# A diffusion transformer block on one core: one load for batch 1's x, one multiply moved up on VectorE, one K step split around a scale group

## The chip, the cores and the metric

The kernel runs on one core of a Trainium2 chip. Its metric is the device time of one execution in microseconds. Before the change, eight runs gave a median of 244.0 us (243.49 to 245.54).

## The reference, cut to what matters

```python
mod = (_silu(c) @ w_mod).reshape(B, 6, 1, D)
shift_a, scale_a, gate_a, shift_m, scale_m, gate_m = [mod[:, i] for i in range(6)]
h = _layernorm(x) * (1 + scale_a) + shift_a
qkv = (h @ wqkv).reshape(B, N, 3, H, Dh)
...
attn = _softmax(jnp.einsum('bqhd,bkhd->bhqk', q, k) * Dh ** (-0.5))
a = jnp.einsum('bhqk,bkhd->bqhd', attn, v).reshape(B, N, D) @ wo
x = x + gate_a * a
h2 = _layernorm(x) * (1 + scale_m) + shift_m
m = _gelu(h2 @ w_fc1) @ w_fc2
return x + gate_m * m
```

Here B is 2, N is 256, D is 1152, H is 2 and the hidden width F is 4608. Everything is bfloat16. All weights together are 50 MB, and each is read once.

## The kernel before, in words

The 512 tokens are four tiles of 128 rows: tiles 0 and 1 are batch 0, tiles 2 and 3 are batch 1. Row p of a partition holds tokens 2p and 2p+1 of a batch, so the two tiles of one batch are the two halves of 4608 contiguous bytes per partition in HBM. D is nine chunks of 128 columns.

All x and weight loads are issued from SyncE's queue (SP), in program order, and start with x in the order tile 0, 1, 3, 2 (L85 and L86), then alternate between column groups of the scale weights `w_scale_a` (L107) and rows of the key weights `w_k` (L104). Transfers take turns on eight completion semaphores, so each one waits for the transfer eight places before it.

The change lies in the first stage, up to about 24 us, which computes the K projection while its inputs still arrive:

- **Warming up.** TensorE runs float32 matmuls on zeros (`warm`, L173).
- **Layer-norm statistics.** Tiles 0 and 2 are done on ScalarE (`act_stats`, L204: two passes with an accumulator); tiles 1 and 3 on VectorE (`stats_piece`, L193: three pieces, then an aggregate, L195). VectorE runs strictly in the order written: tile 1's pieces, the squared mean of tile 0 (L211), tile 3's first piece, tile 0's variance (`act_var`, L222), tile 3's other pieces and aggregate, and then the normalisation `norm1` (L231) of tiles 1, 0 and 3. GpSimd makes the reciprocal square roots of tiles 0, 1 and 3 (`pool_rsqrt`, L327); ScalarE that of tile 2 by logarithm and exponential (`ln_exp_rsqrt`, L227 and L228).
- **Scale.** `scale_group` (L245) multiplies one or more column chunks of `w_scale_a` by silu(c): nine tiny matmuls per chunk. Chunks 0 and 1 are called `pm0` and `pm1`. `scale_add` adds one (L253 on ScalarE, L255 on VectorE).
- **Transposing and modulating.** `transpose_x` (L262) turns normalised chunks with TensorE into PSUM. `modulate` multiplies by the scale on the way to `hT0` (on VectorE L268, or for chunk 0 of batch 0 at L356; on ScalarE L270). For chunks 4 and up, both batches are one PSUM tile; VectorE does batch 0, and ScalarE then does batch 1.
- **K steps.** `k_step(k, c0, c1, m0, m1)` (L278) adds chunk k's contribution to six PSUM accumulators m = 0 to 5, for token columns c0 to c1. For k from 3 on (L387 to L393) the loop does, at k = 3, 5 and 7, the scale group of the next chunks, then the transposes of chunk k+1, then the K step with 512 columns.

After the K steps come panels 6 to 8 of K (L307), the shift (L405), Q (L510), attention, V (L588), the output projection (L679) and the two MLP matmuls (L732 and L788). Every engine's instructions keep the order of the program text, because the kernel ties each to the one before it.

Of the kernel before, what the change touches and what calls it, by code (L numbers as in the profile page):

```python
# [19 lines left out]
def kernel(  # L20
# [11 lines left out]
    nc = tc.nc  # L32
    B, N, D = x.shape
# [4 lines left out]
    T = B * N  # L38
    NT = T // P
    TPB = N // P  # L40
# [19 lines left out]
    def acc_tile(shape, name, dt=FP32):  # L60
        return psum.tile(shape, dt, name=name, tag="acc", bufs=6)
# [5 lines left out]
    x_v = x.rearrange("b (p l) d -> p b l d", l=TPB)  # L67
# [14 lines left out]
    x_sb = act.tile([P, NT, D], BF16, name="x_sb", tag="x_sb")  # L82
    c_sb = act.tile([B * KD, P], BF16, name="c_sb")
    nc.scalar.dma_start(c_sb[:], c_v)
    for t in (0, 1, 3, 2):  # L85
        nc.sync.dma_start(x_sb[:, t, :], x_v[:, t // TPB, t % TPB, :])  # L86

    zeros = const.tile([P, T], BF16, name="zeros")
    nc.vector.memset(zeros[:], 0.0)
# [55 lines left out]
    hT0 = aT  # L145
# [74 lines left out]
    def act_var(t):  # L220
        one = slice(t, t + 1)
        nc.vector.scalar_tensor_tensor(  # L222
            mv1[:, t, 1:2], dsq[:, one], 1.0 / D, dm2[:, one], op0=ALU.mult, op1=ALU.add
        )
# [5 lines left out]
    def norm1(t, c0, c1):  # L230
        nc.vector.tensor_scalar(  # L231
            xns[t][:, c0:c1], x_sb[:, t, c0:c1], mv1[:, t, 0:1], rstd1[:, t:t + 1],
            op0=ALU.subtract, op1=ALU.mult,
        )
# [4 lines left out]
    def scale_group(k0, k1, tile_of=aux_tile):  # L239
        pm = tile_of([P, k1 - k0, B], "pm")  # L240
        for j in range(k0, k1):
            if j == 0:
                nc.tensor.matmul(pm[:, 0, :], ones_row[:], ones_row[:, 0:B], start=True, stop=False)
            for k in range(KD):
                nc.tensor.matmul(  # L245
                    pm[:, j - k0, :], w_scale_a[:, k, j * P:(j + 1) * P], sT[:, k, 0:B],
                    start=(k == 0 and j > 0), stop=(k == KD - 1),
                )
        return pm

    def scale_add(pm, k0, k1, eng="d"):
        if eng == "a":
            nc.scalar.activation(scale_a[:, k0:k1, :], pm[:], ACT.Identity, bias=ones[:])  # L253
        else:
            nc.vector.tensor_scalar_add(scale_a[:, k0:k1, :], pm[:], 1.0)  # L255

    def transpose_x(ks, ts, pt=None, j0=0):
        if pt is None:
            pt = aux_tile([P, len(ks), len(ts) * P], "pt", BF16)
        for j, t in enumerate(ts, j0):  # L260
            for i, k in enumerate(ks):
                nc.tensor.transpose(pt[:, i, j * P:(j + 1) * P], xns[t][:, k * P:(k + 1) * P], ident[:])  # L262
        return pt
# [10 lines left out]
    def k_step(k, c0=0, c1=T, m0=0, m1=KM1):  # L274
        for m in range(m0, m1):
            if k == 0 and c0 == 0:
                pk[m] = acc_tile([P, T], "pk")
            nc.tensor.matmul(  # L278
                pk[m][:, c0:c1], w_k[:, k, m * P:(m + 1) * P], hT0[:, k, c0:c1],
                start=(k == 0 and c0 == 0), stop=(k == KD - 1), skip_group_check=True,  # L280
            )
# [33 lines left out]
    def both(pt, k):  # L315
        for b, e in enumerate("da"):
            modulate(pt, 0, k, b, b * N, e)
# [32 lines left out]
    pt_a = transpose_x([0, 1], BT[0])  # L350
    act_sq_mean(2)
    act_mean(2)
    norm1(3, 0, CUT)
    pm0, pm1 = [scale_group(k, k + 1, acc_tile) for k in range(2)]
    act_var(2)
    nc.vector.tensor_scalar_mul(hT0[:, 0, 0:N], pt_a[:, 0, :], pm0[:, 0, 0:1])  # L356
    scale_add(pm1, 1, 2, "a")
    modulate(pt_a, 1, 1, 0, 0, "d")
    ln_exp_rsqrt(rstd1[:, 2:3], mv1[:, 2, 1:2])
# [25 lines left out]
    k_step(2, 0, N)  # L385
    k_step(2, N, T)
    for k in range(3, KD):  # L387
        if k in (3, 5, 7):
            k1 = min(k + 3, KD)
            scale_add(scale_group(k + 1, k1), k + 1, k1)  # L390
        if k < KD - 1:
            both(transpose_x([k + 1], range(NT)), k + 1)
        k_step(k)  # L393
    for m in range(KM1):
        k_evac(m)

# [446 lines left out]
```

## Time and profile before

| What | Value |
|---|---|
| median of eight runs | 244.0 us (243.49 to 245.54) |
| profiled execution, its own time | 244.49 us |
| its span, first to last instruction | 242.7 us |
| TensorE busy | 237.6 us (98%) |
| VectorE, ScalarE, GpSimd busy | 91.4, 59.7, 29.0 us |
| bytes read from HBM | 50.14 MB |
| mean granted TensorE clock | 1.000 |

Times inside an execution are microseconds from the start of the span. In the timeline, each row is a run of equal instructions on one engine: start, length, engine, source line, operation, output<-inputs, shapes, count, and in brackets the idle time before the first of them with what ended it. In the chain of waits, each row is start, length and what held the end of the program at that time, followed back from the last instruction. "PEld" is TensorE's weight load, "SPq" the issue of a transfer on SyncE's queue.

### The profile page before, as it was taken

The page shows a single profiled execution, that of the slowest core. Times are in us where ns is not written, and L with a number is a line of the kernel's source. Part 1 is how long each engine was busy: PE and PEld are TensorE (multiplying, and loading weights), DVE is VectorE, ACT ScalarE, POOL GpSimd, SP SyncE. Part 2 cuts the span into 40 slices and gives each one's busy share as a digit, 9 for nine tenths or more (in the row PEclk, how much of TensorE's full clock was granted, in tenths as well). Part 3 has the DMA queues.
Part 4 walks back from the last instruction along what each step waited for, and adds up shares of the span by engine and source line. Part 5 has one row for each costly group of instructions (what it writes and reads, how often), then busy time and mean ns, then how long its engine had stood idle before and what let it go on. Part 6 is the DMA issues. An engine that isn't in the chain of part 4 may idle for free.

```text
span 242.7 us, 3999 instructions
## 1 busy us (share of the span) xinstructions
PE 237.6 (98%) x1701; PEld 145.4 (60%) x1701; DVE 91.4 (38%) x193; ACT 59.7 (25%) x120; POOL 29.0 (12%) x48
## 2 busy tenths in 40 slices
PE   8999999999999999999999999999999999999994
PEld 5685444466567665888854444444665665665674
DVE  4652442318416578831001999960010000000001
ACT  6632332307214032672422223332000000000000
POOL 2400000001400333200000000001121121111111
PEclk9999999999999999999999999999999999999999
DMA  6999999998599999239999999999200000000000
GB/s 189 321 318 277 365 367 391 390 393 280 96 320 397 389 375 143 39 66 329 389 392 392 346 326 304 258 326 302 93 20 16 20 16 16 20 16 16 29 23 16
DMA packets 48781, 53.29 MB, mean 220 GB/s; under 512 B 9587, under 2 KB 36475, under 8 KB 48763
## 3 DMA queue, kind: packets, MB, share of 16 engines
q1 hardware_dynamic: 41312, 50.14, 62.3%
q10 hardware_dynamic: 6939, 1.71, 4.9%
q0 software_dynamic: 512, 1.19, 1.7%
q8 instruction: 13, 0.21, 0.4%
q14 instruction: 5, 0.04, 0.1%
HBM read 50.14 MB, written 1.19 MB: 212 GB/s over the span
## 4 chain that ended last, share of the span: by engine, by line
PE 90%; SPq 4%; DMA 3%; issue 0%; DVE 0%; DVEq 0%
PE pacc L732 29%; PE pacc L788 29%; PE pacc L679 7%; PE pacc L588 7%; PE pq L510 7%; DMA w_scale_a<-in_w_mod_dram 3%; SPq L104 3%; PE pk L307 2%; PE pk L278 2%; PE pa L628 2%; PE ps_s L545 2%; PE pn L405 2%; SPq L107 1%; SPq L86 1%; PE pg L487 0%; PE pm L245 0%
## 5 line engine op out<-in xcount | busy, mean ns | idle before, releaser
L732 PE MATMUL pacc<-hT,w_f 128*128 128x256 bf16 (+1 forms) x432 | 70.5, 326 | 0.0
L788 PE MATMUL pacc<-w_f,gT 128*128 128x384 bf16 (+2 forms) x468 | 70.5, 314 | 0.0
L788 PEld LDWEIGHTS <-gT 128*128 128x128 bf16 x468 | 44.4, 98 | 26.2
L732 PEld LDWEIGHTS <-w_f 128*128 128x128 bf16 x432 | 42.2, 98 | 27.6
L794 DVE TENSOR_TENSOR tmp<-pacc,gate 128x384 f32<-128x384 f32 (+2 forms) x13 | 6.9, 527 | 65.6 <-PE pacc L788 57.0
L764 ACT ACTIVATE gT<-pacc 128x512 bf16<-128x512 f32 x24 | 14.4, 598 | 32.6 <-PE pacc L732 32.6
L458 DVE SCALAR_TENSOR_TENSOR part<-w_gate_m,s,part 128x1152 f32<-128x1152 bf16 x16 | 21.3, 1410 | 0.0
L796 POOL TENSOR_TENSOR o_sb<-tmp,x 128x384 bf16<-128x384 f32 (+1 forms) x12 | 11.7, 974 | 53.8 <-DVE tmp L794 53.8
L679 PE MATMUL pacc<-w_o,big 128*128 128x384 bf16 x108 | 17.9, 326 | 0.0
L510 PE MATMUL pq<-hT,w_q 128*128 128x512 bf16 x81 | 17.8, 379 | 0.0
L588 PE MATMUL pacc<-w_v,hT 128*128 128x384 bf16 x108 | 17.7, 326 | 0.0
L588 PEld LDWEIGHTS <-hT 128*128 128x128 bf16 x108 | 10.5, 98 | 7.1 <-issue 0.3
L679 PEld LDWEIGHTS <-big 128*128 128x128 bf16 x108 | 10.4, 98 | 7.2 <-issue 0.4
L510 PEld LDWEIGHTS <-w_q 128*128 128x128 bf16 x81 | 7.8, 97 | 9.5
L278 PE MATMUL pk<-big,w_k 128*128 128x256 bf16 (+1 forms) x72 | 13.2, 326 | 0.1
L685 POOL TENSOR_TENSOR x<-tmp,x_sb 128x384 f32<-128x384 f32 x8 | 7.3, 915 | 27.1 <-DMA w_scale_m<-in_w_mod_dram 15.2
L456 DVE TENSOR_SCALAR part<-w_gate_m,s 128x1152 f32<-128x1152 bf16 x2 | 1.5, 816 | 22.4 <-DMA w_gate_m<-in_w_mod_dram 22.4
L480 POOL DMA_DIRECT2D gates_dram<-nat_v x2 | 1.1, 536 | 67.6 <-DVE nat_v L478 67.6
L278 PEld LDWEIGHTS <-w_k 128*128 128x128 bf16 x72 | 6.7, 98 | 3.8 <-issue 0.4
L173 PE MATMUL pwarm<-zeros 128*128 128x256 f32 x20 | 7.7, 556 | 1.2 <-DVE eps_t L93 1.2
L753 ACT ACTIVATE gT<-pacc 128x512 bf16<-128x512 f32 x12 | 6.5, 599 | 9.1 <-PE pacc L732 9.1
L501 POOL DMA_DIRECT2D gates_dram<-nat x4 | 2.3, 587 | 50.6 <-DVE nat L498 49.9
(101 smaller groups left out, 166.4 us busy)
## 6 DMA issues: line engine op xcount, KB each, us to landing
w_f<-in_w_fc_dram SPq DMA_DIRECT2D x12, 864.0 KB, 14.9
w_f<-in_w_fc_dram SPq DMA_DIRECT2D x3, 1728.0 KB, 8.0
w_f<-in_w_fc_dram SPq DMA_DIRECT2D x2, 2592.0 KB, 17.2
w_gate_a<-in_w_mod_dram SPq DMA_DIRECT2D x3, 864.0 KB, 11.8
w_v<-in_wqkv_dram SPq DMA_DIRECT2D x3, 864.0 KB, 13.9
w_o<-in_wo_dram SPq DMA_DIRECT2D x3, 864.0 KB, 14.1
w_shift_m<-in_w_mod_dram SPq DMA_DIRECT2D x3, 864.0 KB, 8.2
w_scale_m<-in_w_mod_dram SPq DMA_DIRECT2D x3, 864.0 KB, 13.7
```

The costliest lines, as they stand in the source:

```text
L104: nc.sync.dma_start(w_k[:, k0:k1, c0:c1], wqkv_v[:, k0:k1, D + c0:D + c1])
L173: nc.tensor.matmul(dst[:, 0:T // 2], zeros32[:, 0:P], zeros32, start=True, stop=True)
L278: nc.tensor.matmul(pk[m][:, c0:c1], w_k[:, k, m * P:(m + 1) * P], hT0[:, k, c0:c1], start=(k == 0 and c0 == 0), stop=(k == KD - 1), skip_g ...
L458: nc.vector.scalar_tensor_tensor(part[:, b, :], wg[:, k, :], s32[:, k, b:b + 1], part[:, b, :], op0=ALU.mult, op1=ALU.add,)
L510: nc.tensor.matmul(pq[m][:], w_q[:, k, m * P:(m + 1) * P], hT[:, k, :], start=(k == 0), stop=(k == KD - 1), skip_group_check=True,)
L588: nc.tensor.matmul(pacc[:], hT[:, k, t * P:(t + 1) * P], w_v[:, k, pnl * PW:(pnl + 1) * PW], start=(k == 0), stop=(k == KD - 1),)
L679: nc.tensor.matmul(pacc[:], aT[:, k, t * P:(t + 1) * P], w_o[:, k, c0:c1], start=(k == 0), stop=(k == KD - 1),)
L685: (nc.gpsimd if pool_add else nc.vector).tensor_tensor(x1[:, t, c0:c1], tmp[:], x_sb[:, t, c0:c1], op=ALU.add)
L732: nc.tensor.matmul(dst, w_f1[m // KD][:, k, ml * P:(ml + 1) * P], hT[:, k, c0:c1], start=start, stop=(k == KD - 1), **kw,)
L764: nc.scalar.activation(gT[:, m, :], pacc[:], ACT.Gelu_apprx_tanh)
L788: nc.tensor.matmul(pacc[:], gT[:, kk, t * P:(t + 1) * P], w_f2[j][:, r, c0 - n * PW:c0 - n * PW + cw], start=(kk == 0), stop=(kk == KF - 1),)
L796: (nc.vector if last else nc.gpsimd).tensor_tensor(o_sb[:], tmp[:], x1[:, t, c0:c0 + cw], op=ALU.add)
```

## The change

Three edits in the first stage:

1. Tiles 2 and 3 of x, which were two loads of 288 KB (tile 3 first), become one load of 576 KB with 4608 contiguous bytes per partition. Tiles 0 and 1 keep their loads and their place.
2. On VectorE the multiply of chunk 0 of batch 0 (L356) is put before tile 2's variance (L222) instead of after it.
3. In the K loop, the matmuls of K step 5 for accumulators 0 and 1 are put before the scale group of chunks 6 and 7; those for accumulators 2 to 5 stay where they were.

```diff
-    for t in (0, 1, 3, 2):
-        nc.sync.dma_start(x_sb[:, t, :], x_v[:, t // TPB, t % TPB, :])
+    for t in range(TPB):
+        nc.sync.dma_start(x_sb[:, t, :], x_v[:, 0, t, :])
+    nc.sync.dma_start(x_sb[:, TPB:2 * TPB, :], x_v[:, 1, :, :])
...
     pm0, pm1 = [scale_group(k, k + 1, acc_tile) for k in range(2)]
+    nc.vector.tensor_scalar_mul(hT0[:, 0, 0:N], pt_a[:, 0, :], pm0[:, 0, 0:1])
     act_var(2)
-    nc.vector.tensor_scalar_mul(hT0[:, 0, 0:N], pt_a[:, 0, :], pm0[:, 0, 0:1])
     scale_add(pm1, 1, 2, "a")
...
     for k in range(3, KD):
+        split = 2 if k == 5 else 0
+        k_step(k, 0, T, 0, split)
         if k in (3, 5, 7):
             k1 = min(k + 3, KD)
             scale_add(scale_group(k + 1, k1), k + 1, k1)
         if k < KD - 1:
             both(transpose_x([k + 1], range(NT)), k + 1)
-        k_step(k)
+        k_step(k, 0, T, split)
```

## The prediction

> **What bounds the kernel now.** I read the page's chain of waits first, then that chain in order of time, then TensorE's waits, then the timeline of the first 23 us, because all three edits lie there.
>
> ```profile
> PE 90%; SPq 4%; DMA 3%; issue 0%; DVE 0%; DVEq 0%
> ```
>
> TensorE bounds nine tenths of the span; transfers bound only the start. In order of time, the last stretch that is not TensorE is this:
>
> ```profile
> 11.62 8.41 DMA w_scale_a<-in_w_mod_dram
> 20.03 0.05 issue
> 20.08 0.60 PE pm L245 x18
> ...
> 20.93 1.30 PE pk L278 x6
> ```
>
> The scale weights of chunks 6 and 7 land at 20.03, and TensorE waits for them. After that TensorE waits for no transfer: its list of waits from 24 us on is empty. Any shift of TensorE at 22 us therefore reaches the end undiminished. The waits of its first 40 us:
>
> ```profile
> PE pwarm L173 <- DVE eps_t L93: 1.2, 1, 1.2
> PE pm L245 <- DMA w_scale_a<-in_w_mod_dram: 0.7, 2, 0.3
> ```
>
> Two waits for scale weights, one at 9.67 and one at 20.08. The timeline shows what stands behind each:
>
> ```profile
> 6.30 0.56 DVE L193 BATCH_NORM_STATS2 stats<-x_sb 128x6 f32<-128x384 bf16 x1 [0.17 <-DMA x_sb<-in_x_dram]
> ...
> 6.78 0.14 DVE L222 SCALAR_TENSOR_TENSOR mv<-dsq,dm 128x1 f32<-128x1 f32 x1
> ...
> 7.07 0.73 POOL L327 TENSOR_TENSOR rstd<-mv,neg_half 128x2 f32<-128x2 f32 x1 [0.42 <-DVE mv L222]
> 7.71 1.26 ACT L204 ACTIVATE xn<-x_sb 128x1152 bf16<-128x1152 bf16 x1 [1.31 <-DMA x_sb<-in_x_dram]
> ...
> 8.04 0.67 DVE L231 TENSOR_SCALAR xn<-x_sb,mv,rstd 128x512 bf16<-128x512 bf16 x2
> ...
> 8.85 0.38 PE L262 MATMUL pt<-ident,xn 128*128 128x128 bf16 x4
> ...
> 9.67 0.60 PE L245 MATMUL pm<-sT,w_scale_a 128*128 128x2 bf16 x18 [0.33 <-DMA w_scale_a<-in_w_mod_dram]
> ...
> 10.38 0.26 ACT L253 ACTIVATE scale_a<-pm,ones 128x2 f32<-128x2 f32 x1
> ...
> 10.67 0.30 ACT L227 ACTIVATE rstd<-mv,eps_t 128x1 f32<-128x1 f32 x1
> ...
> 11.30 0.41 DVE L231 TENSOR_SCALAR xn<-x_sb,mv,rstd 128x512 bf16<-128x512 bf16 x1
> ...
> 11.77 0.28 PE L262 MATMUL pt<-ident,xn 128*128 128x128 bf16 x2
> ```
>
> Tile 3 lands at 6.28, tile 2 only at 7.69. VectorE starts tile 3's statistics the moment that tile is there, and everything that batch 0 needs (tile 0's variance, its root on GpSimd, the normalisation of tiles 1 and 0) is queued behind them. `pm0` at 9.67 waits for its weights with the transposes done at about 9.2: that path has some 0.45 us to spare.
>
> **Edit 1, one load for tiles 2 and 3.** It removes one issue (0.43 us, with 0.04 between issues) from SP, so every later issue can come 0.47 earlier. I take that as worth nothing: the issue of `w_k` at 5.42 already lasts 2.89 us, the queue pushing back. What it could give is bounded by 0.47 and, since the engines' share was 0.75 and 0.69 between 5 and 6 us, more nearly by 0.3. The eight-semaphore rotation moves up by one place; the transfers now waited for (c, tiles 0 and 1, then the pair) have landed before their waiters are issued. No wait on SP appears.
>
> It adds a wait: tile 3's statistics now wait for tile 2's bytes too. Call the landing of the pair t. Behind it on VectorE, with the rows' own distances from tile 3's 6.28: tile 0's variance at t+0.50, GpSimd's root at t+0.79 to t+1.52, tile 3's remaining statistics until t+1.76, the normalisation of tiles 1 and 0 until t+2.43, the four transposes from t+2.57, then `pm0` at t+2.95. ScalarE's two passes over tile 2 end at t+2.76, as 10.45 follows 7.69 now, before they are needed. So `pm0` moves from 9.67 to t+2.95: a delay d = t - 6.72. From `pm0` on, the distances stay: the weights of chunk 0 and 1 land 1.93 us after x (9.62 after 7.69), well before t+2.95.
>
> What is t? The same bytes, at the same place of the queue, are all there at 7.69 now. Lower end: the slowest part of tile 1 lands at 4.35 by the trace's semaphore records; 589,824 bytes at the page's best 393 GB/s are 1.50 us, so 5.85. Upper end: tile 3's part on the slowest engine took 1.93 us (4.35 to 6.28); two such are 8.21. The gap between 5.85 and 7.69 is slow packets: single ones of 2304 bytes took 0.4 to 1.2 us between 3.7 and 5.5 us, against some 0.1 us else. Half as many packets may meet fewer. The nearest row is 7.69; I take 7.5, so d = +0.78 (ends -0.87 and +1.49).
>
> The Trainium skill, "DMA: Bandwidth & Descriptors", section "Rules for kernel authors", advises to coalesce small transfers into a large one, and its fit for one transfer (2.0 us + bytes/436e3, an estimate here) would land the pair at about 5.0, issued at 1.63, which would be a gain. The trace disagrees in advance: the four x loads already overlap, landing 0.71, 1.93 and 1.41 us apart. The same page, on why a DMA increments its semaphore by 16, says that only the full count means that all data has landed; that is the rule against this edit.
>
> **Edit 2, the multiply before tile 2's variance.** Its input `pm0` is ready at about 10.15, yet it starts at 10.55, behind the variance that waits until 10.48. Moved up, the first K step could start 0.28 earlier (10.68, when TensorE is free, instead of 10.96). But TensorE then stands at tile 2's transposes, 11.77, which hang on ScalarE: its scale add at 10.38 waits for `pm1`, the logarithm at 10.67 follows it. The variance, now behind the multiply's 0.27 us of occupation, is ready for 10.67 still. Worth 0.00; ends: a gain of 0.16 (what TensorE loses before 11.77, 0.27 between starts instead of 0.11) and a loss of 0.35, the multiply's length, if the logarithm had to wait for all of it.
>
> **Edit 3, two matmuls of K step 5 first.** In these rows TensorE finishes K step 4 and waits:
>
> ```profile
> 18.27 1.46 PE L278 MATMUL pk<-big,w_k 128*128 128x512 bf16 x6
> 20.08 0.60 PE L245 MATMUL pm<-sT,w_scale_a 128*128 128x2 bf16 x18 [0.35 <-DMA w_scale_a<-in_w_mod_dram]
> ...
> 22.28 1.46 PE L278 MATMUL pk<-big,w_k 128*128 128x512 bf16 x6
> ```
>
> Six 512-column matmuls take 1.30 from start to start, so the group could have begun at 19.57: 0.51 lost. Two matmuls of 0.216 fill 0.43 of it; their data (chunk 5, ScalarE done at 19.34) is there. A new wait eats some: chunk 6 is transposed by 20.71 (the last start) and modulated by VectorE, then ScalarE, until 21.86. Between those transposes and K step 6 there were 1.57 us of TensorE work; now 1.14, against 1.21 needed. So edit 3 gains 0.43 - 0.07 = 0.36 where the stall is whole, and costs 0.07 where there is none.
>
> **The sum.** TensorE reaches the group at 19.57 + 0.43 + d. With d = 0.78 that is 20.78, later than the weights' 20.03, so no stall is left. K step 6 starts at 20.78 + 1.84 = 22.62 against 22.28: +0.34. On the profiled execution's own 244.49 this is 244.83.
>
> That execution is 0.49 above the median. Its stall explains such a difference: 15 of the 16 parts of that load had landed by 18.86, and one came 1.17 later, on an engine that read 16 KB of instructions from 17.74 for 1.2 us. A run without that collision has no 0.51 to give back; there the change costs 0.78 + 0.07, and 244.0 becomes 244.85. Both give 244.8.
>
> **The rivals.**
>
> Fewer slow packets: t near 6.9, d = +0.18. Then 244.49 + 0.18 - 0.36 or 244.0 + 0.25: about 244.3, no measurable change. For it: half the packets, and 12 of the 16 parts of tile 2 had landed by 7.05. Against it: the slowest engine decides, and it lost 1.7 us.
>
> Faster: the slow packets vanish, t = 5.85, d = -0.87, and every later load moves up with its slowest engine, by about 0.8. On the profiled time that is 244.49 - 0.8 - 0.36 = 243.3. For it: contiguous 4608-byte rows, and the dip of the transfer rate to 184 GB/s between 4.5 and 5 us. Against it: the first scale group that comes too late ends it; chunks 4 and 5 have only 0.28 (landed 15.80, used 16.08). Edit 1 helps only below t = 6.72.
>
> The clock: with t+2.57 for the transposes, TensorE idles from 8.77 to about 10.1. The warm-up matmuls start 0.427 apart until 6.9 and 0.216 apart from 7.3, so the array was at half pace for its first 6 us; as long a relapse would cost 3 us, 247.8. Against it: the stretch from 8.8 to 10.96 is thin already, and the 256-column matmuls after it start 0.109 apart, which is full pace.
>
> **How the numbers follow.** The forecast (t about 7.5, own range 244.5 to 245.4) has 0.42, fewer slow packets 0.36, faster 0.18, the clock 0.04. I take 0.3% (0.73 us) as what a measurement can tell from no change. The forecast lies just past it, and I count nearly all of it as slower, with the clock: 0.44. Same 0.38, faster 0.18. The range reaches down into the faster case, 243.3, and up to the upper end of t, 244.0 + 1.49 + 0.07 = 245.6.
>
> **What would show it.** After the change, VectorE's first piece of tile 3 and ScalarE's pass over tile 2 should start together, at t. `pm0` should start at t + 2.95 with no wait for weights before it: VectorE is late there instead. The multiply L356 should come before the variance, and tile 2's transposes still 2.1 us after `pm0`. The group of chunks 6 and 7 should start without a wait, and K step 6 should start 1.84 us after it. I am wrong if t is below 6.7, if a group waits for weights again, or if 512-column matmuls start 0.43 apart.

## The result, and the profile after

The changed kernel takes 245.39 us (median of 11 runs, 245.1 to 246.9) against 243.92 (median of 32, 243.33 to 245.54). The ratio is 1.0074, with a 95% interval of 1.0058 to 1.0090: it is slower, by about 1.8 us. The forecast was slower by 0.8. The direction is right, the size less than half of what came.

The runs fall into two groups, told apart by the granted TensorE clock, averaged over a run. Of twelve runs listed with their clock, eight had 0.998 to 1.000 and a median of 245.23 (one of them, 244.33, is not among the eleven above; without it the median is 245.29); four had 0.990 to 0.992 and a median of 246.59. Of 92 runs of the kernel before that were made beside the experiments, 89 had 0.998 or more, median 243.83, and three had 0.992 or 0.993 (245.38 to 245.72). So the loss has two parts: 1.40 us at full clock, and 1.36 more in a third of the runs. Together that is 1.40 + 1.36 / 3 = 1.85, against 1.8 by the ratio.

The profiled execution of the changed kernel is one at full clock: its own time is 245.51 and its span 243.7, against 244.49 and 242.7. Its lines are numbered one higher from the loads on, because of the added line. The chain of waits of the changed kernel, by engine:

```profile
PE 94%; DMA 3%; DVE 1%; issue 1%; SPq 0%; ACT 0%; DVEq 0%; ACTq 0%
```

The same chain in order of time (start, length, what held the end of the program), from the start on:

```profile
1.63 6.63 DMA x_sb<-in_x_dram
8.26 0.02 issue
8.29 0.04 DVE stats L194
...
10.28 0.41 DVE xn L232
...
10.83 0.38 PE pt L263 x4
...
11.32 0.55 PE pm L246 x18
```

Before, the chain went through the weights that landed at 20.03. Now the one transfer that holds the end is the load of tiles 2 and 3, issued at 1.63 and landed at 8.26. From there the chain runs through tile 3's statistics and batch 0's normalisation to the first transposes. TensorE's waits in the first 45 us of the changed kernel say the same:

```profile
PE pt L263 <- DVE dm L212: 2.1, 1, 2.1
PE pwarm L174 <- DVE eps_t L94: 1.2, 1, 1.2
PE pt L263 <- DVE xn L232: 0.2, 1, 0.2
```

Both waits for scale weights are gone. In their place stands a wait of 2.1 us for VectorE, before the first transposes. The timeline of the changed kernel:

```profile
8.29 0.56 DVE L194 BATCH_NORM_STATS2 stats<-x_sb 128x6 f32<-128x384 bf16 x1 [2.08 <-DMA x_sb<-in_x_dram]
8.29 1.26 ACT L205 ACTIVATE xn<-x_sb 128x1152 bf16<-128x1152 bf16 x1 [1.97 <-DMA x_sb<-in_x_dram]
8.76 0.14 DVE L223 SCALAR_TENSOR_TENSOR mv<-dsq,dm 128x1 f32<-128x1 f32 x1
...
9.05 0.73 POOL L328 TENSOR_TENSOR rstd<-mv,neg_half 128x2 f32<-128x2 f32 x1 [2.33 <-DVE mv L223]
...
10.02 0.67 DVE L232 TENSOR_SCALAR xn<-x_sb,mv,rstd 128x512 bf16<-128x512 bf16 x2
...
10.83 0.38 PE L263 MATMUL pt<-ident,xn 128*128 128x128 bf16 x4 [2.07 <-DVE dm L212]
...
11.25 0.60 PE L246 MATMUL pm<-sT,w_scale_a 128*128 128x2 bf16 x18
...
13.23 0.28 PE L263 MATMUL pt<-ident,xn 128*128 128x128 bf16 x2 [0.15 <-DVE xn L232]
...
21.46 0.59 PE L246 MATMUL pm<-sT,w_scale_a 128*128 128x2 bf16 x18
...
23.27 1.46 PE L279 MATMUL pk<-big,w_k 128*128 128x512 bf16 x6
```

VectorE's first piece of tile 3 and ScalarE's pass over tile 2 start together, at 8.29. The first scale group starts 2.99 us after the landing and tile 2's transposes at 13.23, which is 1.46 later than before. The group of chunks 6 and 7 starts at 21.46 without a wait, where it waited until 20.08 before. K step 6 starts at 23.27 against 22.28. TensorE's 0.99 us at that place is 0.99 at its last matmul too (240.30 against 239.31). The rest of the span's 1.05 lies behind the last matmul; the last section returns to it.

### The profile page after: what moved, and what is told of

Its sections match the earlier page's. It is cut to its first block, busy times and chain, and to the rows that moved or that the text cites. A ratio compares the mean times of both kernels' runs of the same rounds, so it can differ in the third digit from the quotient of the medians.

```text
span 243.7 us, 3998 instructions
## 1 busy us (share of the span) xinstructions
PE 237.1 (97%) x1701; PEld 145.4 (60%) x1701; DVE 91.5 (38%) x193; ACT 59.7 (24%) x120; POOL 29.0 (12%) x48
## 4 chain that ended last, share of the span: by engine, by line
PE 94%; DMA 3%; DVE 1%; issue 1%; SPq 0%; ACT 0%; DVEq 0%; ACTq 0%
PE pacc L735 29%; PE pacc L791 29%; PE pacc L682 7%; PE pacc L591 7%; PE pq L513 7%; PE pk L279 5%; DMA x_sb<-in_x_dram 3%; PE pk L308 2%; PE pa L631 2%; PE ps_s L548 2%; PE pn L408 2%; PE pt L263 1%; PE pm L246 1%; PE pg L490 0%; DVE stats L194 0%
```

## The experiments

Each experiment was timed beside the kernel before on its chip. The table gives the ratio to it, then the median of the runs with a granted clock of at least 0.995 (count in brackets), how far that lies above the same median of the kernel before on the same chip, and how many runs had less. The kernel before differs from chip to chip, with medians from 243.69 to 244.13 us, so kernels timed on different chips are compared by the difference. For the changed kernel, the difference is to the kernel before on all four chips.

| Kernel | Ratio, 95% interval | us at full clock | Above before, us | Runs below 0.995 |
|---|---|---|---|---|
| before, all four chips | | 243.83 (89) | | 3 of 92 |
| changed | 1.0074 [1.0058, 1.0090] | 245.23 (8) | 1.40 | 4 of 12 |
| edit 1 alone | 1.0095 [1.0066, 1.0124] | 245.18 (4) | 1.38 | 2 of 6 |
| edit 2 alone | 1.0018 [1.0000, 1.0036] | 244.00 (11) | 0.20 | 1 of 12 |
| edit 3 alone | 0.9995 [0.9981, 1.0009] | 243.60 (11) | -0.20 | 0 of 11 |
| edits 2 and 3 | 1.0007 [0.9995, 1.0019] | 243.78 (12) | -0.02 | 0 of 12 |
| four loads, tile 3 last | 1.0034 [1.0018, 1.0051] | 244.49 (10) | 0.80 | 2 of 12 |
| changed, batch 0 first on VectorE | 1.0078 [1.0052, 1.0105] | 245.16 (3) | 1.47 | 3 of 6 |
| changed, 14 warm-ups | 1.0081 [1.0060, 1.0102] | 245.80 (6) | 2.11 | 0 of 6 |
| changed, rows of 2304 bytes | 1.0097 [1.0078, 1.0116] | 246.15 (3) | 2.46 | 3 of 6 |
| changed, spare loads | 1.0043 [1.0021, 1.0065] | 244.42 (7) | 0.60 | 5 of 12 |
| before, spare loads | 0.9997 [0.9981, 1.0013] | 243.87 (12) | 0.05 | 0 of 12 |
| changed, spare loads, 14 warm-ups | 1.0052 [1.0032, 1.0072] | 245.25 (12) | 1.13 | 0 of 12 |
| before, spare loads, edit 3 | 0.9987 [0.9970, 1.0004] | 243.81 (12) | -0.32 | 0 of 12 |

### Which edit: one at a time

The edits are those of the diff, each applied to the kernel before; the fourth kernel is the changed one with this undone:

```diff
-    for t in range(TPB):
-        nc.sync.dma_start(x_sb[:, t, :], x_v[:, 0, t, :])
-    nc.sync.dma_start(x_sb[:, TPB:2 * TPB, :], x_v[:, 1, :, :])
+    for t in (0, 1, 3, 2):
+        nc.sync.dma_start(x_sb[:, t, :], x_v[:, t // TPB, t % TPB, :])
```

> The kernel before with edit 1 alone. Theory A (tile 3's statistics wait for the whole pair, and batch 0's work is queued behind them on VectorE): the first scale group starts 2.95 us after the pair lands, as in the changed kernel, the stall at the scale group of chunks 6 and 7 is gone, and the time is 1.2 to 1.6 us above before, all of the change's loss. Theory B (the loss is in the split K step or in the moved multiply): within 0.4 us of before.

> The kernel before with edit 2 alone. Theory A: the first K step starts about 0.28 us earlier (10.7 instead of 10.96 where the weights land as before), tile 2's transposes stay 2.1 us after the first scale group, and the time is within 0.2 us of before. Theory B: 0.35 us or more slower, because tile 2's variance is held up by the multiply.

> The kernel before with edit 3 alone. Theory A: 0.36 us faster in runs in which the weights of chunks 6 and 7 land as late as 20.03, 0.07 slower in runs without that stall: between -0.36 and +0.07 of before. Theory B (two matmuls do not fill the wait, or the wait for chunk 6 behind K step 5 costs more): 0.3 us or more slower.

> The changed kernel with edit 1 undone: edits 2 and 3 together. Theory A: between -0.4 and +0.1 us of before, so that all of the loss of 1.5 us is edit 1's. Theory B (the edits hurt together, each harmless alone): 0.5 us or more above before.

Edit 1 alone has the whole loss: at full clock 1.38 us above before, against the changed kernel's 1.40, and the low clock in two of six runs as well. In the timeline of edit 1 alone:

```profile
8.00 0.56 DVE L194 BATCH_NORM_STATS2 stats<-x_sb 128x6 f32<-128x384 bf16 x1 [1.84 <-DMA x_sb<-in_x_dram]
...
10.97 0.60 PE L246 MATMUL pm<-sT,w_scale_a 128*128 128x2 bf16 x18
```

The scale group again follows the landing by 2.99 us. Edit 2 alone starts the first K step 1.00 us after the first scale group instead of 1.29, as forecast, and tile 2's transposes stay 2.09 behind it. The time doesn't gain: 0.20 above before. Its interval reaches to a loss of 0.36%, so that a small loss isn't excluded. Edit 3 is within the measurement, alone (0.20 below) and with edit 2 (0.02 below). In the profile of edit 3 alone the weights of chunks 6 and 7 landed at 18.57, so there was no wait to fill. The stall of 0.51 us in the profile before is therefore not in every run.

### Late, or one load?

In the one load, tile 3 is late because it lands with tile 2. Four loads with tile 3 last make it late too:

```diff
-    for t in (0, 1, 3, 2):
+    for t in (0, 1, 2, 3):
```

> The kernel before with its four separate loads in the order tile 0, 1, 2, 3. If being late is all (tile 3 now lands where tile 2 did, about 7.7 us): the first scale group starts 2.95 us after that, about 10.65, and the time is 0.7 to 1.1 us above before. If the one load itself is what hurts (its long rows, one completion for two tiles): within 0.3 us of before.

It lands at 7.33, and the first scale group follows by 3.00:

```profile
7.36 0.56 DVE L193 BATCH_NORM_STATS2 stats<-x_sb 128x6 f32<-128x384 bf16 x1 [1.18 <-DMA x_sb<-in_x_dram]
...
10.33 0.60 PE L245 MATMUL pm<-sT,w_scale_a 128*128 128x2 bf16 x18
```

The time at full clock is 0.80 us above before, and the ratio 1.0034 is 0.83 us with its two low-clock runs: the first expectation held. So about 0.8 us of the 1.40 come from tile 3 waiting in the last place. The other 0.6 go with the one load, which lands later than the last of two (8.26 against 7.33 in the profiles).

### The queue on VectorE

```diff
-    stats_piece(3, 0)
     act_var(0)
     pool_rsqrt(0, 2)
     act_mean(0)
-    stats_piece(3, 1)
-    stats_piece(3, 2)
-    pool_eps(3)
-    pool_rsqrt(3, 4)
     norm1(1, 0, CUT)
     norm1(0, 0, CUT)
+    for j in range(NPD):
+        stats_piece(3, j)
+    pool_eps(3)
+    pool_rsqrt(3, 4)
```

> The changed kernel with VectorE's work for batch 0 (tile 0's variance, the normalisation of tiles 1 and 0) put ahead of tile 3's statistics. If the queue on VectorE carries the loss: the transposes of batch 0 come back to about 8.6 us, the first scale group waits for its weights again (10.3 in the changed kernel's profile), and the time falls 0.6 to 1.0 us below the changed kernel. If the loss is in the transfers alone: within 0.3 us of the changed kernel.

The transposes came back, to 8.64, and the wait for the weights returned, but the time at full clock is 1.47 above before, no better than the changed kernel's 1.40. The timeline of this kernel:

```profile
8.64 0.39 PE L263 MATMUL pt<-ident,xn 128*128 128x128 bf16 x4
...
10.29 0.60 PE L246 MATMUL pm<-sT,w_scale_a 128*128 128x2 bf16 x18 [1.16 <-DMA w_scale_a<-in_w_mod_dram]
...
11.53 0.28 PE L263 MATMUL pt<-ident,xn 128*128 128x128 bf16 x2 [0.39 <-DVE xn L232]
...
12.94 0.28 PE L263 MATMUL pt<-ident,xn 128*128 128x128 bf16 x2 [0.21 <-DVE xn L232]
```

The first scale weights landed only at 10.25, two thirds of a microsecond after the 9.62 of before. Still, the first scale group starts 0.96 earlier than in the changed kernel, while tile 2's transposes start only 0.29 earlier (12.94 against 13.23), and TensorE's last matmul too (240.01 against 240.30). So the weights are not what holds the end up. The chain of waits of this kernel shows what is:

```profile
10.45 0.58 POOL rstd L328
...
11.38 0.35 DVE big L355
11.73 0.08 DVE mv L223
11.83 0.30 ACT rstd L228
...
12.47 0.42 DVE xn L232
...
12.94 0.28 PE pt L263 x2
```

It runs through tile 3's root on GpSimd, the multiply of chunk 0, which VectorE does behind tile 3's normalisation, and then tile 2's variance, root and normalisation. Behind the landing of the pair, the work on tiles 3 and 2 is itself nearly as late as the queue for batch 0. My theory that the queue carries the loss alone fell here.

### Why the one load lands late

Two suspects: its rows of 4608 bytes, and the weights' issue, which the missing load brings forward. The first was tried with 16 unused elements at the end of each tile's row on chip, so that the same load moves rows of 2304 bytes:

```diff
-    x_sb = act.tile([P, NT, D], BF16, name="x_sb", tag="x_sb")
+    x_sb = act.tile([P, NT, D + 16], BF16, name="x_sb", tag="x_sb")
...
-    nc.sync.dma_start(x_sb[:, TPB:2 * TPB, :], x_v[:, 1, :, :])
+    nc.sync.dma_start(x_sb[:, TPB:2 * TPB, 0:D], x_v[:, 1, :, :])
```

> The changed kernel with x laid out in rows of 1168 elements on chip, so that the one load moves rows of 2304 bytes instead of 4608. If the long rows are what made the pair land at 8.26 instead of 7.69: it lands at 7.7 or before, and the time falls 0.4 to 0.7 us below the changed kernel. If the length of the rows does not matter: within 0.2 us of it.

It landed at 8.32, so shorter rows alone didn't bring it earlier. Its time at full clock is 2.46 above before, 1.1 more than the changed kernel, so neither expectation on the time held. That is from three runs, and why this layout costs more is open.

The second suspect was tried by two spare loads of 4.5 KB, into a tile that nothing reads, behind x:

```diff
     nc.sync.dma_start(x_sb[:, TPB:2 * TPB, :], x_v[:, 1, :, :])
+    for _ in range(2):
+        spare = act.tile([B * KD, P], BF16, name="spare", tag="spare", bufs=2)
+        nc.sync.dma_start(spare[:], c_v)
```

> The changed kernel with two spare loads of c (4.5 KB each, into a tile that nothing reads) on SP between x and the first scale weights, so that the scale and key weights are issued about 0.9 us later. In four profiles with the one load its last part lands at 7.8 to 8.3, in five with two loads at 7.2 to 7.7, though the median part lands earlier. If the weights' issue, which the one load brings forward by 0.47 us, is what holds up a few engines: the last part lands at 7.5 or before, and the time falls by 0.5 us or more below the changed kernel in runs at full clock (245.1 to 245.5). If it is the one load itself: last part at 7.8 to 8.3 again, time within 0.3 us.

> The kernel before with the same two spare loads. If the weights' issue holds the engines up: its last x lands before 7.2, the first scale weights no later than 9.3, and the time is 0.2 us or more below before, a version faster than both. If not: the weights land as before or up to 0.5 us later, and the time is within 0.3 us of before or above it.

The weights were issued 0.76 us later (2.86 instead of 2.10), and x landed 0.9 earlier, at 7.35. The timeline of the changed kernel with spare loads:

```profile
7.37 0.56 DVE L197 BATCH_NORM_STATS2 stats<-x_sb 128x6 f32<-128x384 bf16 x1 [1.29 <-DMA x_sb<-in_x_dram]
...
10.34 0.60 PE L249 MATMUL pm<-sT,w_scale_a 128*128 128x2 bf16 x18
```

Its time at full clock is 0.60 above before, that is 0.8 less than the changed kernel's 1.40. So the first expectation held for it. The trace's semaphore records show 16 landings for each of these loads; I call them its parts. Over all profiles but that of the last run of this section:

| Kernel | first scale weights issued | last x load: median part | last part | first scale weights landed |
|---|---|---|---|---|
| two loads for batch 1 (5 profiles) | 2.56 to 2.57 | 6.22 to 6.37 | 7.23 to 7.71 | 9.25 to 9.70 |
| one load (changed, edit 1 alone, batch 0 first, 14 warm-ups) | 2.10 | 5.68 to 5.98 | 7.79 to 8.29 | 9.78 to 10.27 |
| one load, rows of 2304 bytes | 2.34 | 6.30 | 8.32 | 10.26 |
| one load, spare loads (2 profiles) | 2.86 to 2.87 | 5.60 | 7.32 to 7.35 | 9.44 to 9.45 |
| two loads, spare loads (2 profiles) | 3.32 to 3.35 | 5.80 to 5.92 | 6.60 to 6.75 | 8.58 to 8.71 |

The typical part of the one load does land earlier than with two loads, but a few parts land a microsecond or more behind the others: in the changed kernel three parts came after 8.2, thirteen before 7.3. In both kernels the spare loads put the weights' issue some 0.8 us later, and the last part landed earlier. That fits the issue as the cause, but doesn't show it alone: the spare loads also put two small transfers in between, and with rows of 2304 bytes an issue 0.24 later went with no earlier landing. How a part is held up is not visible in the trace. In the kernel before, x landed 0.6 to 1.0 us earlier but the time gained nothing (0.05 above before): of the first expectation the landings held and the time did not. More on that below.

One more run asked whether batch 1's place in memory matters:

```diff
-    for t in (0, 1, 3, 2):
+    for t in (3, 2, 0, 1):
```

> The kernel before with the four tiles of x loaded in the order 3, 2, 0, 1; only the landings are of interest, the time will be above before. In all profiles so far the loads in the first two places land with their parts within 0.7 us of each other, those in the last two places spread over 1.5 us or more. If the place in the order decides: tiles 0 and 1 now spread over 1.3 us or more. If batch 1's place in memory decides: tiles 3 and 2 do.

Tiles 3 and 2, now first, landed with their parts 0.7 and 0.5 us apart; tile 0, third, 0.65; tile 1, last, 2.0. So it is not batch 1's place in memory. In this one run (246.38 us) the load in the last place has the spread, though it is tile 1, but the one in the third place hasn't (0.65, against 1.49 in the profile before).

### The clock

> The changed kernel with six more warm-up matmuls (14 instead of 8) before the first transposes, 1.3 us at full pace. In four of twelve runs of the changed kernel the granted clock was 0.990 to 0.992 and the time 246.5 to 246.9, in the others 0.998 to 1.000 and 244.3 to 245.5. If TensorE's idle time of 2.4 us before the transposes is what lowers the clock: no run below 0.995, all between 244.3 and 245.6. If the clock has another cause: still about a third of the runs at 0.99 and above 246.3.

The edit is the number of float32 warm-up matmuls ahead of the first transposes, in the changed kernel and then in the one with spare loads:

```diff
-    warm(8, pwarm)
+    warm(14, pwarm)
```

> The changed kernel with the two spare loads and with 14 warm-up matmuls instead of 8. With 8, five of twelve runs had a granted clock of 0.991 to 0.993 and took 245.6 to 246.1, the other seven 244.4 to 244.5. If TensorE's idle time before the transposes is the cause: no run of twelve below 0.995. If not: again about five at 0.99. In either case runs in which the array reaches full pace late may take up to 1 us more, because the warm-up matmuls then run into the transposes.

With 14 none of 18 runs had the low clock; with 8, 17 of 42 runs of kernels with the one load had it. So work for TensorE ahead of the transposes takes the low clock away. Idle time just before them isn't needed for it: in the profile with batch 0 first on VectorE the transposes start at 8.64 and TensorE waits 1.16 us after them instead, yet three of six runs of that kernel had the low clock. More warm-ups are no cure as they stand: the times at full clock are 0.5 to 0.7 us higher with them and spread from 245.08 to 246.34 and from 244.64 to 246.21, where 245.6 at most was expected of the first. I put that down to runs in which the array reaches its full pace late, so that the extra matmuls hold the transposes up; no profile shows one of these runs.

By luck the profile of the kernel with short rows was of a run with the low clock (0.993). Stretches of it; after the five engines' busy times (instructions in brackets) come the granted clock (PEclk), the DMA share and GB/s:

```profile
9.00:11.00 2.00, 0.10 (x2) 0.13 (x3) 1.80 (x6) 1.97 (x4) 1.66 (x4) 1.00 1.13 345
11.00:12.00 1.00, 1.00 (x24) 0.79 (x23) 0.68 (x2) 0.08 (x1) 0.45 (x2) 0.80 1.11 327
12.00:13.00 1.00, 1.00 (x5) 0.52 (x4) 0.68 (x4) 0.69 (x4) 0.00 (x0) 0.50 1.12 323
13.00:14.00 1.00, 1.00 (x7) 0.72 (x5) 0.24 (x1) 0.00 (x0) 0.00 (x0) 0.50 1.14 308
14.00:15.00 1.00, 1.00 (x8) 0.75 (x7) 0.37 (x2) 0.00 (x0) 0.00 (x0) 0.50 1.10 322
15.00:16.00 1.00, 1.00 (x11) 0.90 (x10) 0.69 (x2) 0.47 (x1) 0.00 (x0) 0.99 1.12 325
```

and TensorE's timeline in it:

```profile
10.90 0.38 PE L263 MATMUL pt<-ident,xn 128*128 128x128 bf16 x4 [3.16 <-DVE dm L212]
...
12.82 1.49 PE L279 MATMUL pk<-big,w_k 128*128 128x256 bf16 x6
```

TensorE had no work for 3.16 us before 10.90, and from 11.60 to 15.01 the array was given half its clock by the trace's clock records. Six 256-column matmuls took 1.28 from the first to the next instruction (12.82 to 14.10) instead of 0.65. The Trainium skill, "TensorE: Matmul & The Clock Gate", section "Part 1: The HAM clock gate", says that the array drops to half pace after an idle window of about 3.4 us, and that the windows run free of the kernel. This case agrees on the length and on the free run: the stretch at half pace was 3.41 us long, and the array reached full pace anywhere from 4.6 to 7.8 us in the profiles. It differs on one point, as the stretch ahead of the drop was not all idle. Counted on in steps of 3.41 us from where full pace began (4.77), the step from 8.19 to 11.60 held 0.70 us of TensorE's work. In the other fourteen profiles, counted the same way, none of the steps up to 16 us held less than 1.60 us of work, and none had a drop; in the changed kernel the idle time fell into two steps, with 1.91 and 2.69 us of work. So the same idle time can fall into one step in some runs and over two in others.

### A version faster than both?

```diff
     # the kernel before with two spare loads behind x, and:
     for k in range(3, KD):
+        split = 2 if k == 5 else 0
+        k_step(k, 0, T, 0, split)
...
-        k_step(k)
+        k_step(k, 0, T, split)
```

> The kernel before with the two spare loads and edit 3. In the profile with the spare loads alone the first scale group started at 8.96 instead of 9.67 and the K steps 0.95 us earlier, yet the median stayed at 243.87. If the wait for the scale weights of chunks 6 and 7 takes that gain back in most runs: with the split K step 0.2 us or more below before. If the gain is lost elsewhere: within 0.15 us of the spare loads alone.

It isn't told from before: at full clock it is 0.32 below before on its chip, which is what the first expectation asked for, but the ratio's interval reaches from 0.9970 to 1.0004. The spare loads alone were 0.05 above before and edit 3 alone 0.20 below, neither told from it. No tried kernel is clearly faster than the kernel before. In the profile with spare loads alone, the last matmul starts at 237.93, against 238.42 in the profile of edit 3 alone, which also had no stall at the scale group. But the span ends 3.75 us after it, against 3.37. That takes 0.38 of 0.49 back.

## Why the prediction was right or wrong

- **Where the change acts: right.** The profile after has the wait that edit 1 was said to add, at the place it was said to stand, with the distances said: 2.99 us from landing to the first scale group (2.95 forecast). Tile 2's transposes come 1.98 after that group (2.10), K step 6 comes 1.81 after the group of chunks 6 and 7 (1.84).
- **The landing t of the pair: mis-sized, and the step that failed.** I took 7.5, with ends at 5.85 and 8.21, and argued that half as many packets may meet fewer slow ones. It measured 8.26 in the profile after and 7.79 to 8.32 in five profiles of kernels with the one load and no spare loads. With 8.26 the forecast's own sum gives d = 1.54 and +1.10 at K step 6; TensorE moved by 0.99. For a run without the stall the sum gives 1.54 + 0.07 = 1.61; at full clock the loss is 1.40. The rival with fewer slow packets is refuted at its condition: the median part did come earlier, but the last part decides.
- **The earlier issue on SP, "worth nothing": wrong in sign.** I bounded what it could give (0.3 to 0.47 us) and not what it could take. With the spare loads, which put the issue 0.76 us later (the change brought it forward by 0.47), about 0.8 us came back. As far as the runs show, the mis-sized t is largely this term; that the issue time alone does it stays open.
- **The queue on VectorE: right in the profile, too simple as a cause.** Taking the queue away brought the first scale group forward by 0.96 us but tile 2's transposes by only 0.29, because the work on tiles 3 and 2 behind the landing was nearly as late, and no gain in time could be told.
- **Edit 2 at 0.00 and edit 3 at 0.36 or -0.07: not refuted.** Both are within the measurement. The 0.05 us wait for chunk 6 behind the split K step is in the trace: K step 6 starts 0.107 after the last transpose instead of 0.056. That runs without the stall exist, as argued from the median, is borne out by edit 3's profile. That the late part of this load was on the engine that read instructions is not shown: the trace names no engine for either.
- **The clock: chance and price wrong.** I gave it 4 in 100 and 3 us. It came in 17 of 42 runs of the kernels with the one load and 8 warm-ups, and costs 1.36 in the changed kernel (1.9 with edit 1 alone, but 0.2 with short rows, which stays open). I take the price to be under 3 because half pace lasted one stretch of 3.41 us, in which much of the work is small, and the prediction took one as long as the first 6 us. My ground against it, that the matmuls after the thin stretch ran at full pace, was one execution of a thing that varies from run to run. In the sum over runs it is 0.45 us of the 1.8.
- **The page's fit for one transfer** would have given a landing of about 5.0; the page states it for transfers issued from GpSimd, and this load was issued from SyncE. None of the 16 parts landed before 5.29 in any profile with the one load.

## What to carry to other kernels

Merging two loads makes the first user of either wait for the last part of both, so ask what is queued behind that user, on its engine, before counting the saved issue. A transfer issued earlier may hold up the ones before it, as seems to be the case here, so bound its effect from both sides. Where a change adds idle time to TensorE near the start (here 2.1 us in the changed kernel's profile and 3.2 in that with short rows), look for two times over the runs, which one profile won't show; list the granted clock of every run.

## What I had not expected of the hardware

- With two spare loads ahead of them, the first weights were issued 0.76 us later; x landed 0.9 us earlier, and the weights themselves 0.8 earlier (9.44 instead of 10.27). With two loads for batch 1, the same moved x from 7.23 to 7.71 down to 6.60 to 6.75, and the weights from 9.25 to 9.70 down to 8.58 to 8.71.
- The end of the program depends on how many loads come before it. There SP waits for the completion semaphores one after the other, some 0.06 us each by the trace. In the kernel before, two such waits are left when the last output lands, with one load less three, and with two loads more eight: from the last matmul to the end of the span it is 3.37, 3.44 and 3.75 us. With one load more in all (the changed kernel with spare loads) one wait is left, and it is 3.33 us. That is 0.07 us of the change's loss, which no step of the prediction held.
- The array's half clock lasted 3.41 us in the one profile that caught it, after a step of the same length with 0.70 us of work in it, and the clock was full again from 15.01 on.
